# Squares in four listed slots, decays in six, and the last batch's input transposed before its gate: a gated recurrence and a gated convolution on one Trainium2 core

## Chip, cores, metric

One core of a Trainium2 chip. The metric is device time in microseconds (us). The engines are PE (TensorE, with PEld its weight loads), DVE (VectorE), ACT (ScalarE), POOL (GpSimd) and SP (SyncE, which here only issues DMAs). An operation is named by a short word and its numbers, as in the kernel's own list: `sc.25.0` is the scan of chunk 25, half 0.

## What is computed

x, r_gate and i_gate are [4, 6336, 256] in float32, with four small parameter arrays. Cut to what matters:

```python
a_t = exp(8 * sigmoid(r_gate) * log(sigmoid(a_param)))
x_gated = sqrt(max(1 - a_t * a_t, 1e-6)) * sigmoid(i_gate) * x
for t in range(S):                      # per batch row, all 256 channels
    h = a_t[:, t] * h + x_gated[:, t]
    y[:, t] = h
gate = sigmoid(causal_conv5(y, conv_w))  # depthwise, 5 taps
out = (gate * (y @ w_val)) @ w_out
```

## The kernel before

The 25,344 rows of the four sequences are one line of time. It is cut into 51 **windows** of 512 rows (the first two and the last have 256), and the windows into 28 **chunks**, mostly two windows each: chunk 24 is windows 45 and 46, chunk 25 is 47 and 48, chunk 26 is 49, chunk 27 is 50. Chunks are gathered in eight **batches** (`BATCHES`, L19), because the square root needs another table of ACT than tanh and exp: each batch costs two table loads. The last batch is chunks 25, 26 and 27.

Rows arrive with time on the partitions; the recurrence needs channels on the partitions, in two halves of 128 (`h`). For a chunk `c` or a window `w` the steps are:

- `lr`, `li`, `lx` (L279): SP loads a window of the r gate, the i gate and x, 512 KB each, into rings of four windows.
- `ta`, `tb` (L297, L300, ACT): tanh of half the gate, from which the sigmoid comes.
- `tr` (L344, PE) transposes tanh of the r gate, `ex` (L360, ACT) takes exp of it: the **decay** a_t, in float32, in `aring`.
- `sq` (L368, POOL) or `sa` (L376, ACT) squares the decay into `ering`. `rt` (L393, ACT) takes the square root of 0.25 - 0.25 a^2 over a whole batch, in as few instructions as there are contiguous pieces, and writes it as bf16 over the front half of the same piece.
- `pp` and `up` (L307, L319, POOL): 1 + tanh, and its product with x, written to `uring` in time-major order. For a few windows PE copies x to PSUM instead (`xp`, L324) and DVE does both steps in one (`uv`, L333).
- `nt` (L407, PE) transposes the root back to time-major order in PSUM; `xg` (L414, DVE) multiplies `uring` by it; `xt` (L422, PE) transposes the product, pairs of bf16 moved as one float32 word, to channel-major order in PSUM; `sc` (L444, DVE) scans it with the decays into `yring`.
- `cv` (L456, PE) is the convolution, 20 small matmuls a window; `tg` (L463, ACT) its tanh; `vl` (L471, PE) is y @ w_val; `gv` (L476, DVE) the gated product; `ou` (L486, PE) its product with w_out; `cd` (L494, DVE) or `ca` (L496, ACT) copies it to SBUF, `st` (L507) stores it.

So in the last batch the way from the root to the scan goes `rt`, `nt`, `xg`, `xt`, `sc`. The lines that say it (L411 to L427 and L430, shortened):

```python
def op_xg(c):
    ...
    nc.vector.tensor_tensor(out=u, in0=live.pop(("nT", c)).bitcast(BF16), in1=u, op=ALU.mult)
...
def op_sc(c, h):
    xT = live.pop(("xT", c, h)).bitcast(BF16)
```

**What sets the order.** `ORDER` (L35 to L98) is a list of 980 words written out ahead of time; the loop at L518 emits them one by one. Every engine takes its own instructions in the order of the list, and waits where data or a buffer are not ready. The numbers after an @ are the PSUM banks, eight in all, that a word uses. So a word that is moved in the list is moved on its own engine's queue, past what else stands there.

**The rings.** `aring` holds 5120 columns of each half, five chunks of 1024, used in turn. `ering` also holds 5120, and `places` (L138) hands out its slots in turn as well. A square can be written only when the root or the `nt` that used its slot has gone by.

Of the kernel before, what the change touches and what calls it, by code (L numbers as in the profile page):

```python
# [20 lines left out]
NA = 5120  # L21
NE = 5120
# [13 lines left out]
s_ident s_small s_kt s_diag lr.0 lr.2 lr.1 li.0 lr.3 ta.0 ta.2 lr.4 tr.0.1@5 ta.1 tr.2.0@4 ex.0.1 lr.5 tr.1.1@0  # L36
tr.2.1@7 ex.2.0 lr.6 sq.0.1 ex.1.1 li.2 ex.2.1 tr.0.0@0 tb.0 tr.1.0@7 ex.1.0 li.4 ex.0.0 lx.1 sq.1.0 ta.3 s_wl.3 sq.2.0
lx.0 li.3 sq.0.0 lx.3 ta.4 sq.1.1 li.1 sq.2.1 lx.2 lr.8 tb.2 tr.3.1@0,1 ex.3.1 tr.3.0@6,7 li.6 lr.9 xp.0@3 lr.7 uv.0
lx.4 ex.3.0 sq.3.1 s_wl.0 s_wl.2 tb.3 sq.4.1 lr.10 tb.1 xp.2@4,5 sq.3.0 xp.1@0 s_wl.1 uv.1 rt.0.0 li.8 sq.4.0 li.5 pp.3
nt.0@6 rt.1.0 nt.1@7 lx.6 xg.1 pp.4 xg.0 xt.0.1@2 sc.0.1 up.3 uv.2 xt.1.1@2 xt.1.0@3 nt.2@6 xg.2 up.4 lx.7 sc.1.1 lx.5  # L40
xt.2.0@7 ta.5 xt.0.0@0 xt.2.1@6 li.7 sc.0.0 nt.3@4,5 sc.1.0 s_wcast ta.6 xg.3 lr.11 cv.0@2,3 lr.12 sc.2.1 cv.1@4,5 tg.0
lr.14 tb.4 sc.2.0 lr.13 tr.5.1@0,1 vl.0@2,3 gv.0 tg.1 li.10 pp.6 ex.5.1 li.9 xt.3.1@4 lx.8 sc.3.1 up.6 tr.5.0@2,3
cv.2@6,7 ex.5.0 xt.3.0@1 pp.5 sc.3.0 tb.5 up.5 nt.4@2,3 vl.1@4,5 tg.2 gv.1 sq.5.0 lx.9 xg.4 ou.0.0@4 ta.7 li.11
ou.1.0@7 li.12 cd.1.0 xt.4.0@2 sq.6.1 cd.0.0 cv.3@6,7 ta.8 sc.4.0 st.0 lr.16 pp.7 st.1 tg.3 tr.7.0@0,1 lr.17 xt.4.1@5
up.7 ex.7.0 sc.4.1 vl.2@6,7 xp.8@2,3 tb.6 sq.5.1 lx.11 cv.4@0,1 gv.2 tg.4 uv.8 tr.7.1@4,5 li.14 sq.6.0 lr.15 ex.7.1
ou.2.0@6,7 lx.10 lr.18 vl.4@2,3 sq.7.0 cv.5@0,1 gv.4 tb.7 cd.2.0 sq.8.0 vl.3@4,5 tg.5 gv.3 xp.9@2,3 sq.7.1 lx.13 uv.9
ou.4.0@0,1 li.15 lx.12 rt.2.0 ou.3.0@4,5 li.13 sq.8.1 cd.3.0 vl.5@6,7 gv.5 pp.10 cd.4.0 ou.5.0@6,7 rt.2.1 up.10 cd.5.0
st.4 nt.5@4,5 xg.5 nt.6@2,3 pp.11 lx.14 li.16 xg.6 xt.5.1@0 pp.12 st.2 xt.5.0@6 st.3 sc.5.1 xt.6.1@7 up.11 cv.6@4,5
ta.10 sc.5.0 up.12 nt.7@2,3 ta.9 lr.21 lr.22 vl.6@0,1 tg.6 xg.7 lr.20 lx.15 tb.8 lr.19 sc.6.1 tr.9.0@4,5 xt.6.0@6 tb.9
li.18 tr.9.1@2,3 pp.14 lx.16 gv.6 xt.7.1@7 li.17 pp.13 ex.9.1 sc.7.1 li.19 cv.7@0,1 up.14 st.5 li.20 ex.9.0 sc.6.0  # L50
pp.15 vl.7@2,3 up.13 tg.7 ou.6.0@4,5 ta.12 cv.9@6,7 cd.6.0 up.15 gv.7 xt.7.0@4 tg.9 lr.25 lr.26 vl.8@0,1 sc.7.0 ta.11
st.6 pp.16 cv.8@2,3 lx.18 lx.17 sq.9.0 lx.19 tg.8 tr.11.0@6,7 ex.11.0 vl.9@4,5 gv.8 up.16 ou.7.0@2,3 gv.9 tb.10
nt.8@0,1 cd.7.0 sq.11.0 tr.11.1@6,7 xg.8 st.7 ex.11.1 ou.8.0@2,3 lx.20 pp.17 cd.8.0 xt.8.0@4 xt.8.1@5 sq.10.1 tb.11
cv.11@0,1 sc.8.1 st.8 lr.23 cv.10@2,3 lr.24 sq.10.0 tg.11 li.21 li.22 sc.8.0 tg.10 li.23 ou.9.0@0,1 sq.11.1 ta.14
cv.12@6,7 cd.9.0 sq.9.1 tg.12 lr.30 vl.11@4,5 gv.11 vl.12@2,3 pp.20 vl.10@0,1 gv.12 rt.3.0 sq.12.1 xp.18@4,5 gv.10
# [36 lines left out]
sq.27.0 pp.49 sc.24.1 cv.44@2,3 tg.43 pp.48 pp.50 vl.42@0,1 up.48 gv.42 rt.7.0 ou.41.0@6,7 vl.43@4,5 cd.41.0 up.47
# [10 lines left out]
def kernel(  # L103
# [82 lines left out]
    with tc.manual_schedule():  # L186
# [368 lines left out]
```

## Time and profile before

| | |
|---|---|
| median of 3 runs | 291.31 us (291.29 to 292.64) |
| the profiled execution: its time, its span | 293.39 us, 291.6 us |
| ACT busy in the span | 272.4 us (93%) |
| PE, DVE, POOL busy | 244.7, 243.5, 235.2 us (84, 83, 81%) |
| DMA | 104.75 MB, mean 359 GB/s |
| last root (chunks 25 to 27) | 261.26 to 264.45 us |
| last copy to SBUF ends, span ends | 288.13, 291.6 us |

The span is what the profiler shows of one execution, and that execution's own time is 1.8 us longer. All times in us below are positions in the span unless they are called the time. "Busy" counts overlapping instructions of one engine once. A row's mean is the mean duration of one instruction, which on ACT overlaps its neighbour a little: the sum of all rows' means of ACT is 285.8 us for 272.4 us busy. In a timeline a row merges neighbours of a kind; the bracket is the idle time before it and who ended it.

### The profile page before, as it was taken

What the parts mean: (1) busy time and instruction counts of PE and PEld (TensorE: products, weight loads), DVE (VectorE), ACT (ScalarE), POOL (GpSimd) and SP (SyncE); (2) the same over time, 40 slices, a digit from 0 to 9 for tenths busy, and PEclk for the clock granted to TensorE, in tenths of its full rate; (3) what the DMA queues carried; (4) which work ended last, traced back from release to release, by engine and by line L of the source; (5) the groups of instructions that cost most, each with busy time, mean ns of one, the idle gap of its engine ahead of it and who ended that gap; (6) DMA issues with size and microseconds to landing.
All of it is one profiled execution on the core that took longest, in us unless ns stands there. A gap on an engine that the chain in (4) does not pass through costs nothing. (4 is left out here: it accounts for less than half of the span.)

```text
span 291.6 us, 6228 instructions
## 1 busy us (share of the span) xinstructions
PE 244.7 (84%) x2482; PEld 168.5 (58%) x2507; DVE 243.5 (83%) x201; ACT 272.4 (93%) x191; POOL 235.2 (81%) x156
## 2 busy tenths in 40 slices
PE   1366697988689888899788789899999899999993
PEld 1242565556547456666457567566666577757662
DVE  2001799789999989998899989999999999999980
ACT  6799989999999999999999999999999999997663
POOL 1529949999599899999998999998999966898000
PEclk9997689999999999999999999999999999999999
DMA  7999999998999999899999999999999987782725
GB/s 239 316 386 405 383 407 385 380 371 333 395 411 418 416 415 366 285 418 416 418 416 416 411 411 416 419 388 378 416 416 420 415 326 276 267 288 110 290 87 239
DMA packets 29995, 104.75 MB, mean 359 GB/s; under 512 B 3335, under 2 KB 3854, under 8 KB 29966
## 3 DMA queue, kind: packets, MB, share of 16 engines
q1 hardware_dynamic: 29952, 104.35, 91.7%
q8 instruction: 19, 0.31, 0.4%
q14 instruction: 10, 0.08, 0.1%
q10 hardware_dynamic: 14, 0.01, 0.0%
HBM read 78.39 MB, written 25.95 MB: 358 GB/s over the span
## 5 line engine op out<-in xcount | busy, mean ns | idle before, releaser
L444 DVE TENSOR_TENSOR_SCAN yring<-aring,yring,banks 128x1024 bf16<-128x1024 f32 (+5 forms) x54 | 106.8, 1993 | 2.6 <-PE banks L422 1.3
L368 POOL TENSOR_TENSOR ering<-aring 128x1024 f32<-128x1024 f32 (+2 forms) x55 | 92.6, 1709 | 16.4 <-ACT aring L360 16.3
L319 POOL TENSOR_TENSOR uring<-tbring,xring 128x1024 bf16<-128x1024 bf16 (+1 forms) x45 | 95.3, 2136 | 1.5 <-DMA xring<-in_x_dram 0.8
L476 DVE SCALAR_TENSOR_TENSOR tgring<-tgring,banks 128x1024 bf16<-128x1024 bf16 (+1 forms) x51 | 59.3, 1181 | 7.8 <-PE banks L471 2.8
L456 PE MATMUL banks<-yring,diag 64*64 64x512 bf16 (+7 forms) x1080 | 63.2, 365 | 1.4 <-DVE tgring L476 0.4
L307 POOL TENSOR_SCALAR tbring<-tbring 128x1024 bf16<-128x1024 bf16 (+1 forms) x45 | 46.2, 1039 | 14.9 <-ACT tbring L300 14.8
L486 PE MATMUL banks<-wo,tgring 128*128 128x256 bf16 x396 | 50.5, 273 | 8.9 <-DVE tgring L476 6.2
L463 ACT ACTIVATE tgring<-banks 128x1024 bf16<-128x1024 f32 (+1 forms) x51 | 50.2, 1007 | 4.2 <-PE banks L456 4.1
L360 ACT ACTIVATE aring<-banks,khf 128x2048 f32<-128x2048 bf16 (+3 forms) x34 | 53.4, 1610 | 0.7 <-POOL ering L368 0.3
L471 PE MATMUL banks<-yring,wv 128*128 128x512 bf16 (+7 forms) x191 | 48.4, 359 | 4.9 <-ACT aring L360 1.6
L486 PEld LDWEIGHTS <-tgring 128*128 128x128 bf16 x396 | 42.3, 114 | 17.5 <-DVE tgring L476 7.6
L297 ACT ACTIVATE taring<-rring 128x2048 bf16<-128x2048 f32 (+2 forms) x28 | 47.7, 1722 | 1.9 <-DMA rring<-in_r_gate_dram 1.9
L300 ACT ACTIVATE tbring<-iring 128x2048 bf16<-128x2048 f32 (+2 forms) x28 | 48.0, 1727 | 0.3 <-DVE uring L333 0.3
L456 PEld LDWEIGHTS <-diag 64*64 64x64 bf16 x1080 | 30.3, 107 | 25.2 <-issue 9.7
L393 ACT ACTIVATE ering<-ering 128x2048 bf16<-128x2048 f32 (+4 forms) x11 | 44.1, 4042 | 0.1
L344 PE MATMUL banks<-ident_b,taring 128*128 128x128 bf16 x396 | 29.9, 230 | 12.0 <-ACT taring L297 8.3
L494 DVE COPY oring<-banks 128x1024 f32<-128x1024 f32 (+1 forms) x31 | 36.3, 1182 | 3.6 <-PE banks L486 3.5
L422 PE MATMUL banks<-ident,uring 128*128 128x128 f32 x198 | 30.8, 283 | 7.8 <-DVE uring L414 4.4
L344 PEld LDWEIGHTS <-taring 128*128 128x128 bf16 x396 | 25.5, 103 | 17.6 <-ACT taring L297 10.2
L471 PEld LDWEIGHTS <-wv 128*128 128x128 bf16 x216 | 19.5, 97 | 23.4 <-issue 10.0
L414 DVE TENSOR_TENSOR uring<-banks,uring 128x2048 bf16<-128x2048 bf16 (+2 forms) x28 | 30.2, 1092 | 2.5 <-PE banks L407 2.1
L422 PEld LDWEIGHTS banks<-ident,uring 128*128 128x128 f32 x198 | 22.0, 142 | 16.3 <-DVE uring L414 7.6
(37 smaller groups left out, 139.6 us busy)
## 6 DMA issues: line engine op xcount, KB each, us to landing
rring<-in_r_gate_dram SPq DMA_DIRECT2D x48, 512.0 KB, 8.2
iring<-in_i_gate_dram SPq DMA_DIRECT2D x48, 512.0 KB, 9.8
xring<-in_x_dram SPq DMA_DIRECT2D x48, 512.0 KB, 8.2
out_dram<-oring SPq DMA_DIRECT2D x48, 512.0 KB, 8.2
rring<-in_r_gate_dram SPq DMA_DIRECT2D x3, 256.0 KB, 3.8
iring<-in_i_gate_dram SPq DMA_DIRECT2D x3, 256.0 KB, 6.3
xring<-in_x_dram SPq DMA_DIRECT2D x3, 256.0 KB, 6.9
out_dram<-oring SPq DMA_DIRECT2D x3, 256.0 KB, 7.1
```

The lines of the kernel that those rows point to most:

```text
L300: nc.scalar.activation(**tangent(c, tbring, NTI, iring, NII))
L319: nc.gpsimd.tensor_tensor(out=u, in0=t1, in1=xt, op=ALU.mult)
L344: nc.tensor.transpose(out=bank[:, o:o + P], in_=taring[:, place(w, NTR), j, h * P:(h + 1) * P], identity=ident_b[:])
L360: nc.scalar.activation(out=dst, in_=src, func=ACT.Exp, scale=khf[:, h:h + 1], bias=khf[:, h:h + 1])
L368: nc.gpsimd.tensor_tensor(out=e, in0=a, in1=a, op=ALU.mult)
L422: nc.tensor.transpose(out=bank[:, o + q:o + wins[w] // 2:nq], in_=uring[:, (w + 1) % NU, q, h * P:(h + 1) * P, :].rearrange("p d two -> p ...
L444: nc.vector.tensor_tensor_scan(out=yring[:, h, col:col + o1 - o0], data0=aring[:, h, a_at[c] + o0:a_at[c] + o1], data1=xT[:, o0:o1], initi ...
L456: nc.tensor.matmul(out=gp[oh * 64:oh * 64 + 64, h, a:b], lhsT=diag[half * 64:half * 64 + 64, h, k, :], rhs=yring[half * 64:half * 64 + 64, ...
L463: nc.scalar.activation(out=tgring[:, w % NTG, :, 0:wins[w]], in_=live.pop(("gp", w))[:, :, 0:wins[w]], func=ACT.Tanh, scale=0.5)
L471: nc.tensor.matmul(out=val[:, m, a:b], lhsT=wv[:, hk, m * P:(m + 1) * P], rhs=yring[:, hk, col:col + b - a], start=(hk == 0), stop=(hk == ...
L476: nc.vector.scalar_tensor_tensor(out=tgring[:, w % NTG, :, 0:wins[w]], in0=tgring[:, w % NTG, :, 0:wins[w]], scalar=1.0, in1=live.pop(("va ...
L486: nc.tensor.matmul(out=ops[:, j * D:(j + 1) * D], lhsT=gv[:, hk, j:wins[w]:J], rhs=wo[:, hk, :], start=(hk == 0), stop=(hk == H - 1))
```

## The change

Four things are changed at once.

1. The ring of squares shrinks from five slots to four (`NE` 5120 to 4096), and the slots are listed (`SQUARES_AT`) and not handed out in turn. A batch of four chunks uses all four; a root now covers at most two neighbouring slots (`NPIECE`), so the batches 4, 5 and 7 take two root instructions where they took one. The root's result lies in the front slot of its pair.
2. The ring of decays grows from five chunks to six (`NA` 5120 to 6144). Both rings together take the same space.
3. For the chunks from 25 on (`DIRECT`) there is no `nt`. `xt` transposes the input before it is multiplied by the root, both halves in one word, and leaves it in PSUM; `xg` multiplies it there by the root, which is channel-major already, and writes the product to `uring` in SBUF; `sc` scans from SBUF.
4. `ORDER` is written anew throughout, 977 words. Counted by kind: `xp`/`uv` 6 to 3, `pp`/`up` 45 to 48 each, `nt` 28 to 25, `sq` 55 to 54, `sa` 1 to 2, `ca` 20 to 17, `cd` 31 to 34, `rt` 11 to 14. The table loads stay 14.

```diff
-NA = 5120
-NE = 5120
+NA = 6144
+NE = 4096
+NPIECE = 2048
+DIRECT = 25
+SQUARES_AT = [0, 256, 512, 2048, 3072, 1024, 0, 3072, 2048, 1024, 0, 3072, 2048, 1024, 0, 3072, 2048, 1024, 0, 3072,
+    2048, 1024, 0, 3072, 2048, 1024, 3072, 3584]
-    e_at = places(NE, clen)
+    e_at = SQUARES_AT
...
-            cs, got, k = BATCHES[b], [], 0
+            cs, got, k = sorted(BATCHES[b], key=lambda c: e_at[c]), [], 0
-                while m < len(cs) and e_at[cs[m]] == e_at[cs[m - 1]] + clen[cs[m - 1]]:
+                while m < len(cs) and e_at[cs[m]] == e_at[cs[m - 1]] + clen[cs[m - 1]] and e_at[cs[m]] % NPIECE:
...
+        def u_of(c):
+            u0, nw = (cwins[c][0] + 1) % NU, len(cwins[c])
+            return uring[:, u0:u0 + nw, 0:wins[cwins[c][0]] // (2 * P)].rearrange("p w q d two -> p (w q d two)")
+
         def op_xg(c):
+            u = u_of(c)
+            if c < DIRECT:
+                nc.vector.tensor_tensor(out=u, in0=live.pop(("nT", c)).bitcast(BF16), in1=u, op=ALU.mult)
+                return
+
+            o = 2 * live["n", c]
+            nc.vector.tensor_tensor(out=u, in0=live.pop(("uT", c)).bitcast(BF16),
+                                    in1=ering[:].bitcast(BF16)[:, o:o + H * clen[c]], op=ALU.mult)
+            for h in range(H):
+                live["xT", c, h] = u[:, h * clen[c]:(h + 1) * clen[c]]
...
+        def op_xt(c, *at):
+
+            if c < DIRECT:
+                h, b = at
+                words(c, h, banks[:, b])
+                live["xT", c, h] = banks[:, b].bitcast(BF16)
+                return
+            ps = banks[:, at[0]:at[-1] + 1].rearrange("p b n -> p (b n)")[:, 0:clen[c]]
+            for h in range(H):
+                words(c, h, ps[:, h * clen[c] // 2:(h + 1) * clen[c] // 2])
+            live["uT", c] = ps
```

The parts of the two lists that the prediction speaks of. Before, ACT's order up to the first root, and all words from the last root on:

```text
ta.0 ta.2 ta.1 ex.0.1 ex.2.0 ex.1.1 ex.2.1 tb.0 ex.1.0 ex.0.0 ta.3 ta.4 tb.2 ex.3.1 ex.3.0 tb.3 tb.1 rt.0.0
...
rt.7.0 ou.41.0 vl.43 cd.41.0 up.47 ou.42.0 gv.43 st.41 cv.45 cd.42.0 up.49 nt.25 tg.45 xg.25 vl.45 tg.44 vl.44 gv.45 up.50
xt.25.1 gv.44 ou.43.0 ca.43.0 ou.45.0 sc.25.1 xt.25.0 ca.45.0 st.43 ou.44.0 st.45 cv.46 ca.44.0 st.42 sc.25.0 st.44 tg.46
vl.46 nt.26 nt.27 xg.26 cv.47 xg.27 gv.46 xt.26.1 tg.47 xt.26.0 sc.26.1 vl.47 ou.46.0 sc.26.0 xt.27.1 ca.46.0 cv.48 gv.47
st.46 cv.49 tg.48 sc.27.1 tg.49 vl.48 xt.27.0 gv.48 ou.47.0 ca.47.0 sc.27.0 vl.49 gv.49 st.47 ou.48.0 cv.50 ca.48.0 tg.50
ou.49.0 st.48 ca.49.0 vl.50 gv.50 st.49 ou.50.0 ca.50.0 st.50
```

After, the same two parts:

```text
ta.0 ta.1 ex.0.0 ta.2 tb.0 ex.1.1 ex.0.1 ex.2.1 ex.1.0 ta.3 ex.2.0 ta.4 tb.2 tb.1 ex.3.0 ex.3.1 tb.3 ta.5 rt.0.0
...
xt.25 rt.7.0 gv.41 sq.26.1 vl.43 cv.45 up.49 gv.43 rt.7.1 xg.25 ou.42.0 cv.44 cd.42.0 tg.45 sc.25.1 ou.41.0 st.42 xt.26
ca.41.0 vl.45 tg.44 st.41 gv.45 vl.44 tb.27 vl.46 pp.50 xg.26 up.50 gv.44 ou.43.0 cv.46 ca.43.0 sc.25.0 st.43 tg.46 ou.44.0
ca.44.0 ou.45.0 gv.46 cv.48 ca.45.0 st.44 sc.26.1 cv.47 tg.48 sc.26.0 xt.27 tg.47 ou.46.0 xg.27 ca.46.0 sc.27.1 vl.48
sc.27.0 st.46 vl.47 gv.48 st.45 cv.49 gv.47 tg.49 ou.48.0 ca.48.0 vl.49 gv.49 st.48 ou.47.0 cv.50 ca.47.0 tg.50 ou.49.0
st.47 ca.49.0 vl.50 gv.50 st.49 ou.50.0 ca.50.0 st.50
```

More of the change, by code (lines that the diff above doesn't have):

```diff
@@ L39 @@
[L39 to L43, printed above, removed]
@@ new lines @@
+lr.6 tr.2.0@1 ex.1.1 tr.1.0@5 li.2 tr.2.1@6 ex.0.1 li.1 ex.2.1 sq.0.1 lx.0 ex.1.0 li.3 sq.1.1 ta.3 s_wl.1 sq.0.0 li.4
+pp.0 sq.2.1 ex.2.0 lr.7 s_wl.3 ta.4 sq.2.0 lr.8 lx.2 tb.2 tr.3.0@2,3 lx.1 up.0 tb.1 sq.1.0 lr.9 ex.3.0 tr.3.1@4,5 lx.3
+s_wl.0 ex.3.1 sq.4.0 s_wl.2 lr.10 tb.3 sq.3.1 lx.4 ta.5 li.6 sq.4.1 li.8 li.5 pp.1 xp.2@4,5 sq.3.0 rt.0.0 lx.6 uv.2
+li.7 lr.11 pp.3 rt.1.0 nt.2@7 lr.12 up.1 nt.0@4 nt.1@0 xg.0 xg.2 pp.4 lx.5 xg.1 xt.1.1@2 xt.1.0@7 up.4 xt.0.1@0
+xt.2.0@3 sc.0.1 xt.0.0@6 sc.0.0 sc.1.0 up.3 ta.6 nt.3@0,1 sc.1.1 cv.0@6,7 sc.2.0 lr.13 s_wcast tg.0 xg.3 lr.14
@@ new lines @@
+tr.5.1@4,5 tb.4 xt.2.1@6 cv.1@2,3 sc.2.1 xt.3.1@1 tg.1 li.10 pp.6 sc.3.1 ex.5.1 lx.7 cv.2@2,3 li.9 pp.5 lx.8 up.6 tg.2
+vl.0@4,5 vl.1@0,1 gv.0 tb.5 xt.3.0@7 gv.1 up.5 tr.5.0@2,3 sc.3.0 ou.0.0@6 ta.7 li.12 vl.2@0,1 li.11 ou.1.0@4 sq.5.1
+cd.0.0 ex.5.0 lr.15 gv.2 nt.4@6,7 sq.6.1 cd.1.0 cv.3@0,1 ta.8 xg.4 st.1 cv.4@4,5 sq.5.0 tg.3 lr.18 xt.4.0@6 lr.17 tg.4
+sc.4.0 lr.16 tr.7.1@2,3 sq.6.0 st.0 ex.7.1 lx.9 xp.7@4,5 pp.8 uv.7 tb.6 tr.7.0@0,1 up.8 xt.4.1@4 sc.4.1 ex.7.0
+ou.2.0@6,7 li.14 pp.10 vl.4@2,3 lx.12 lx.10 tb.7 li.13 gv.4 sq.8.0 cv.5@4,5 lx.11 cd.2.0 tg.5 vl.5@0,1 sq.7.1 ta.10
@@ new lines @@
+sc.15.1 ex.19.1 st.22 up.32 vl.24@4,5 lr.42 xt.16.0@7 ta.21 gv.24 vl.26@2,3 sq.20.0 cv.25@0,1 sc.16.0 tb.19 lr.44
+cv.27@4,5 lr.41 sq.19.1 lx.36 li.37 gv.26 tg.25 ou.24.0@6,7 li.40 sq.19.0 tg.27 cd.24.0 vl.27@0,1 xt.16.1@3 gv.27 st.24
+sq.20.1 vl.25@6,7 lr.43 rt.5.0 sc.16.1 ou.26.0@4,5 pp.34 ou.27.0@0,1 pp.33 gv.25 up.33 cd.27.0 rt.5.1 nt.17@2,3 cd.26.0
+ou.25.0@6,7 up.34 lx.37 cd.25.0 nt.18@4,5 xg.17 cv.30@0,1 pp.36 lx.38 li.39 xg.18 xt.17.0@6 tg.30 pp.35 xt.17.1@7
+sc.17.0 cv.29@2,3 ta.22 up.36 cv.28@4,5 tg.29 lr.46 sc.17.1 up.35 st.25 vl.30@0,1 tg.28 lr.45 tr.21.0@2,3 tb.20
@@ new lines @@
+nt.19@4,5 gv.30 ex.21.0 vl.28@6,7 li.41 pp.38 xg.19 st.27 tr.21.1@0,1 li.42 pp.37 gv.28 lx.39 vl.29@4,5 ex.21.1 lx.40
+sq.22.0 xt.18.1@3 gv.29 st.26 cv.31@6,7 sc.18.1 ta.23 up.38 xt.18.0@5 ou.28.0@0,1 tg.31 cd.28.0 vl.31@2,3 up.37 tb.21
+gv.31 ou.29.0@6,7 nt.20@0,1 sc.18.0 sq.22.1 ta.24 li.43 cv.32@2,3 st.28 pp.39 tg.32 lr.50 xg.20 ou.31.0@4,5 li.44
+ca.29.0 pp.40 cd.31.0 vl.32@2,3 tb.22 st.29 sq.21.0 tr.23.1@6,7 lx.42 gv.32 xt.19.0@5 st.31 lr.47 ex.23.1 sc.19.0
+ou.30.0@0,1 up.40 cv.33@2,3 tg.33 xt.19.1@7 cd.30.0 pp.42 lx.44 sa.21.1 tr.23.0@4,5 up.39 sc.19.1 st.30 ex.23.0
@@ new lines @@
+ou.32.0@2,3 li.46 cv.34@0,1 lx.41 cd.32.0 tg.34 sq.23.0 vl.33@6,7 xt.20.1@5 tb.23 gv.33 cv.36@0,1 pp.41 sc.20.1
+cv.35@6,7 ta.27 li.48 sq.23.1 li.47 tg.35 ou.33.0@2,3 cd.33.0 tg.36 vl.34@4,5 pp.43 vl.35@6,7 gv.34 st.33 sq.24.0
+xt.20.0@1 li.45 st.32 gv.35 rt.6.0 lx.43 ou.34.0@4,5 sq.24.1 sc.20.0 ou.35.0@2,3 vl.36@6,7 up.42 ca.35.0 gv.36
+nt.21@0,1 rt.6.1 cd.34.0 up.41 lx.46 nt.22@6,7 xg.21 st.34 cv.38@4,5 lr.48 pp.44 lr.49 xg.22 xt.21.1@0 xt.21.0@1 up.44
+sc.21.1 cv.37@2,3 tg.38 ou.36.0@6,7 up.43 lx.48 tg.37 sc.21.0 tr.27.1@0 lx.45 vl.37@4,5 ca.36.0 tb.24 st.36 gv.37 st.35
@@ new lines @@
+nt.23@6,7 xt.22.1@1 xt.22.0@3 xg.23 tb.25 pp.46 cv.39@4,5 sc.22.1 up.46 tg.39 ou.37.0@6,7 ex.27.1 cv.40@4,5 ca.37.0
+sc.22.0 pp.48 lx.50 li.49 tg.40 pp.45 lx.47 vl.38@0,1 xt.23.0@7 ta.25 sq.27.1 gv.38 vl.40@2,3 pp.47 tr.27.0@6 gv.40
+vl.39@4,5 ex.27.0 up.45 ta.26 tr.25.1@6 gv.39 ex.25.1 ou.38.0@0,1 tr.26.0@2 sc.23.0 ex.26.0 nt.24@4,5 sq.25.1 ca.38.0
+tr.25.0@6 ex.25.0 ou.39.0@2,3 st.38 xg.24 xt.23.1@7 lx.49 ca.39.0 sq.25.0 ou.40.0@0,1 sc.23.1 tr.26.1@6 ca.40.0
+xt.24.0@2 xt.24.1@3 ex.26.1 st.40 cv.41@0,1 up.48 li.50 tb.26 sc.24.0 st.37 cv.42@6,7 tg.41 st.39 up.47 cv.43@4,5
@@ L148 @@
     a_at = places(NA, clen)
-    e_at = places(NE, clen)
+    e_at = SQUARES_AT
+    assert all(e + n <= NE for e, n in zip(e_at, clen))
     segs, y_at, y_wrap = [], [], []
@@ L409, in op_nt, with words @@
             live["nT", c] = bank[:, 0:k]
+        def u_of(c):
+            u0, nw = (cwins[c][0] + 1) % NU, len(cwins[c])
+            return uring[:, u0:u0 + nw, 0:wins[cwins[c][0]] // (2 * P)].rearrange("p w q d two -> p (w q d two)")
         def op_xg(c):
-            u0, nw = (cwins[c][0] + 1) % NU, len(cwins[c])
-            u = uring[:, u0:u0 + nw, 0:wins[cwins[c][0]] // (2 * P)].rearrange("p w q d two -> p (w q d two)")
-            nc.vector.tensor_tensor(out=u, in0=live.pop(("nT", c)).bitcast(BF16), in1=u, op=ALU.mult)
-        def op_xt(c, h, at):
-            bank = banks[:, at]
+            u = u_of(c)
[7 more added lines that the diff above has]
+                live["xT", c, h] = u[:, h * clen[c]:(h + 1) * clen[c]]
+        def words(c, h, out):
             for w in cwins[c]:
@@ L422, in op_xt @@
                     nc.tensor.transpose(
-                        out=bank[:, o + q:o + wins[w] // 2:nq],
+                        out=out[:, o + q:o + wins[w] // 2:nq],
                         in_=uring[:, (w + 1) % NU, q, h * P:(h + 1) * P, :].rearrange("p d two -> p (d two)")
```

93 lines of the change are left out of this document (33 added, 60 removed).

## Prediction

> **What bounds the kernel now.** I read the page's busy times first, then the stretches, the waits, the timeline of the tail and the chain that ended last.
>
> ```profile
> PE 244.7 (84%) x2482; PEld 168.5 (58%) x2507; DVE 243.5 (83%) x201; ACT 272.4 (93%) x191; POOL 235.2 (81%) x156
> ```
>
> ACT has least room, but this is an average over unlike stages, so I cut the span: the middle, and the tail from the start of the last root.
>
> ```profile
> 49.45:261.26 211.81, 190.22 (x2016) 131.96 (x2030) 200.25 (x153) 210.46 (x140) 197.40 (x123) 1.00 0.98 383
> 261.26:288.20 26.94, 25.19 (x251) 16.99 (x252) 22.58 (x21) 18.59 (x17) 7.29 (x4) 1.00 0.49 198
> ```
>
> The columns are time, then busy time of PE, PEld, DVE, ACT, POOL, then PE's granted clock, the DMA's share, GB/s. In the middle ACT is busy 210.5 of 211.8 us: it sets the pace. DVE has 11.6 us of room, POOL 14.4; the DMA's share is 0.98. In the tail ACT has room and PE has not: 25.2 of 26.9, DVE 22.6. The timeline shows the turn:
>
> ```profile
> 261.26 3.19 ACT L393 ACTIVATE ering<-ering 128x3584 bf16<-128x3584 f32 x1
> ...
> 264.77 1.23 PE L407 MATMUL banks<-ident,ering 128*128 128x128 f32 x8
> ...
> 266.11 1.23 DVE L414 TENSOR_TENSOR uring<-banks,uring 128x2048 bf16<-128x2048 bf16 x1 [0.35 <-PE banks L407]
> ```
>
> The root's way through `nt` to `xg.25` takes 4.85 us (261.26 to 266.11), yet DVE waits only 0.35 for it: it had other work. So the shorter way (no `nt`) is worth little as latency. What counts is work taken from PE, and when ACT reaches the last root. The chain that ended last is PE alone from 237.3 to 286.0, which agrees.
>
> **The change, part by part.** Durations are row means; for a queue I sum them and scale by what the queue took (neighbours overlap): ACT 210.5 us for 222.3 of means, 0.947; DVE 0.961; POOL 0.983.
>
> *Start.* ACT's first root moves behind `ta.5` (one 1.92 us tanh); against that stand waits of 1.89, 0.18 and 0.32 us in this stretch, the first (for `lr.6`) mostly filled by `ex.2.0`, and ACT's order otherwise holds the same work. I put the root at 27.5 (26.07 before). `xp.0`, `xp.1` go, so PE has only `xp.2` behind it, and I count its next transposes at the slow row:
>
> ```profile
> 28.21 0.60 PE L407 MATMUL banks<-ident,ering 128*128 128x128 f32 x4
> ...
> 31.52 1.06 PE L407 MATMUL banks<-ident,ering 128*128 128x128 f32 x4
> ...
> 34.48 1.91 PE L407 MATMUL banks<-ident,ering 128*128 128x128 f32 x8
> ```
>
> Four take 0.60 us when PE had just been busy for 4.54 us with `xp` (granted clock 0.98 there) and 1.06 at a clock of 0.50 later. Root to 29.4, eight such to 31.4, products 32.5, then transposes of 0.33 each and five scans to about 36.4, `cv.0` 1.28: `tg.0` at 37.7, as before (37.66). Then nine ACT instructions, 13.1 us before; with about 0.9 of waiting of `tg.1` and `tg.2` for late convolutions `ta.8` ends at 51.7 (before 47.02 + 3.73 = 50.75): **+1.0 us**, and -0.5 if the clock is full. DVE, by the same walk, has done `xg.4` at 50.9. The Trainium skill (TensorE: Matmul & The Clock Gate, What's actually happening) has PE at half rate until about 3.4 us of sustained work; the clocks here agree, and by it the slow row is right for this start.
>
> The doubled POOL work for windows 0 and 1 (`pp` 0.62, `up` 1.18 each, 3.6 us) falls into POOL's early idle time (6.43 and 5.49 us of waits for ACT's exp).
>
> *Middle, ACT.* From `ta.8` to the last root ACT has less to do: four copies fewer ahead of it (12 to 8, -4.1), `tb.27` now behind it (-0.66), two root pieces more (a root is 0.20 + 0.835 per 1000 columns by its rows 1906 and 7035 ns: +0.4), `sa.21.1` and `sa.27.0` for `sa.26.1`. No row has a Square of 1024 or 256 columns: the first lies between 0.73 (512 columns) and 1.24 (exp of 1024), the second between 0 and 0.57 (exp of 256); taken 1.17 and 0.50, together +0.9. Sum -3.4, by 0.947 **-3.3 us** (ends -3.9 and -3.2). So the last root starts at 51.7 + 207.3 = 259.0 (261.26).
>
> *What may not follow.* DVE loses three `uv` pairs (1.47 for a pair or two short ones) less one gained, and gains three copies of 1.22. With no waiting it would reach the last root's place at 250.6 before (49.45 + 209.3 x 0.961), 10.7 ahead of ACT, and at 50.9 + 210.4 x 0.961 = 253.1 after, 5.9 ahead of 259.0. It loses 4.8 us of lead; ACT's tanh then waits more often for convolutions. Nothing shows how much: ends 0 and 4.8, I take a quarter, **+1.2**, because ACT waited under 1 us in the middle with the lead it had.
>
> POOL gains in the middle `pp` and `up` of one window (3.2) less a square (1.9). Its idle time there came in waits for `tb` after roots (4.74, 3.50 us), and the new order puts `tb` nearer to the root: cover enough. With four slots a next batch's squares can't begin before the root, but the root frees the back slot of each pair at once; the list puts them later still: nothing. The loads must come 2 us earlier; the DMA ran at 333 to 385 GB/s from 44 to 73 us and at 326 or less from 233 us on, against 416 at best: nothing.
>
> *Tail.* From the last root on PE had 25.05 us by the chain's pieces (`ou` 0.87, `vl` 0.86, `cv` 1.21, a transpose of `nt` 0.122, of `xt` 0.14). `nt` goes (14 x 0.122 = -1.7), `xt.25` is ahead of the root (-1.1), `cv.44` behind it (+1.2): 23.4, **-1.6 us**. The rest of 26.87 us from the root to the last copy (1.8) and the store behind it (3.5) I leave. The root comes in two parts, so `xg.25` needs 1.9 us of it, not 3.2. The scans from SBUF: every scan in the trace reads PSUM (2338 ns); those of chunks 25 to 27 are 8.5 us together. Bounds from the nearest rows: `xg` at 1215 ns for 2048 shows that DVE has no general loss with an operand in PSUM, so between -0.3 (0.05 each) and +0.3; taken 0.
>
> Sum: +1.0 - 3.3 + 1.2 - 1.6 = **-2.7 us**. The profiled execution would take 290.7 where it took 293.39; its time was 2.1 above the median, so from the median 291.31 - 2.7 = **288.6 us**.
>
> **Rivals.**
>
> *DVE takes over the bound* (slower). After 50.9 it has 232.9 x 0.961 = 223.8 us to do, 222.8 after 49.45 before, and then 1.3 us of `ou.50` and copy remain. Before, it waited 14.5 us on the way, mostly under 1 us at a time for its own last product to come back through PE, which the change does not shorten. With the same waits the last copy ends at 50.9 + 223.8 + 14.5 + 1.3 = 290.5, +2.4: 293.7. It decides once DVE's waits pass 12.1 us. For it: the waits are by PE and ACT after DVE's own results. Against it: DVE had 11 us in hand because ACT was slow.
>
> *All of it comes through*: clock full at the start, no loss of DVE's lead: -0.5 - 3.3 - 1.6 = -5.4, 285.9. Against it: the clock rows.
>
> *Only the tail comes*: the lost lead eats the middle: -1.6, 289.7.
>
> *POOL is late for `xt.25`*. That word now stands ahead of `vl.43` on PE and needs `up.47` and `up.48`. POOL can reach the end of `up.47` at 38.8 (its weight casts' end: 36.1 before, plus most of the four early instructions added) + 213.0 x 0.983 = 248.2 plus its waits; with the 13.7 us of before that is 261.9, 2.9 after the root, and PE stands: -2.7 + 2.9, 291.5. For it: PE takes its queue in order. Against it: the nearer `tb`.
>
> *DVE and POOL exclude each other in the tail.* The scans from SBUF read two SBUF tiles, which no scan before did, and `up.49` (2.16 us) and `up.50` (1.18) may run beside them: up to 3.3 us, of which DVE's room against PE in the tail (25.2 less 21.6 of work and 1.3 behind it, some 2) covers most: +1.3, 289.9. No row shows such a pair in the middle, for or against. The Trainium skill (SBUF — State Buffer, Who interferes with whom) says that a DVE instruction with two SBUF inputs blocks against a GpSimd one that reads SBUF; by that rule it would happen wherever they overlap.
>
> **How the numbers follow.** Forecast 0.37, with 287.4 to 290.0 as its own range; DVE bound 0.20; all comes through 0.13; only the tail 0.12; POOL late 0.10; exclusion 0.08. About 0.5% (1.46 us) is what a measurement of this kernel can tell from no change: below 289.85 is faster, above 292.77 slower. Faster: 0.34 of the forecast, 0.13, half of the tail case and of the exclusion: 0.57. Slower: 0.20. Same: the rest, 0.23. The range runs from the middle of "all comes through" to nearly that of "DVE bound", 286.0 to 293.4, leaving out some 0.07 below and 0.11 above.
>
> **What would show it.** In the changed profile: the first root near 27.5 and `ta.8`'s end near 51.7; the last root near 260 in two pieces; PE busy over 23 us between it and the last copy, in 25; DVE's waits after 51 us at 8 to 11. I am wrong if ACT shows waits of several us in the middle (DVE bound), if PE waits at `xt.25` on POOL, or if scans of the last chunks or `up.50` take well over their rows.

## Result and the profile after

| | before | after |
|---|---|---|
| median of 20 runs each, interleaved | 293.0 us | 291.16 us |
| ratio, 95% interval | | 0.9938 (0.9914 to 0.9961) |
| profiled execution: time, span | 293.39, 291.6 us | 291.52, 289.7 us |

The changed kernel is faster by 0.6%, 1.84 us between the medians and 1.87 between the profiled executions (the interval does not reach 1, but the gain is small). Forecast were 2.7. (The three runs of before that were shown first lie in the lower part of its twenty; that is why 291.16 stands so near to the 291.31 of the prediction.) The size alone misleads, though: two of the three parts of the sum came out on the other side of zero from the forecast. In the experiments below a median is over all runs of a kernel, a ratio over the runs in the faster of the two states that its executions show.

| us in the span | before | after | forecast |
|---|---|---|---|
| first root starts | 26.07 | 26.00 | 27.5 |
| `tg.0` starts | 37.66 | 34.72 | 37.7 |
| `ta.8` ends | 50.75 | 47.81 | 51.7 |
| last root starts | 261.26 | 260.43 | 260.2 |
| last copy ends | 288.13 | 286.76 | |
| start: up to `ta.8` | | -2.94 | +1.0 |
| middle: `ta.8` to the last root | 210.51 | 212.62, +2.11 | -2.1 |
| tail: last root to the last copy | 26.87 | 26.33, -0.54 | -1.6 |
| store behind it | 3.47 | 2.94, -0.5 | 0 |

The middle of before, cut at the end of `ta.8` (columns as in the prediction):

```profile
50.75:261.26 210.51, 188.93 (x1994) 131.30 (x2017) 198.95 (x152) 209.16 (x140) 196.10 (x122) 1.00 0.98 383
```

The busy times of after, then its middle and its tail:

```profile
PE 240.9 (83%) x2485; PEld 163.7 (57%) x2485; DVE 243.2 (84%) x200; ACT 271.1 (94%) x192; POOL 240.5 (83%) x161
```

```profile
47.81:260.43 212.62, 189.91 (x1987) 129.90 (x1984) 201.40 (x152) 206.36 (x138) 200.05 (x122) 0.99 0.99 386
260.43:286.76 26.33, 24.49 (x257) 15.09 (x255) 21.61 (x21) 20.20 (x20) 5.30 (x5) 1.00 0.45 181
```

ACT's work in the middle fell nearly as forecast, from 209.2 us busy to 206.4 (-2.8 for -3.3). The stretch grew all the same: ACT now stands idle 6.3 us in it, 1.4 before. The waits tell where. ACT in the timeline of after:

```profile
113.43 2.06 ACT L364 ACTIVATE aring<-banks,khf 128x2048 f32<-128x2048 bf16 x1 [0.68 <-DVE yring L469]
...
174.67 2.06 ACT L364 ACTIVATE aring<-banks,khf 128x2048 f32<-128x2048 bf16 x1 [2.18 <-DVE yring L469]
...
182.75 1.02 ACT L488 ACTIVATE tgring<-banks 128x1024 bf16<-128x1024 f32 x1 [1.03 <-PE banks L511]
```

and DVE in the same places, with what it was waiting for itself:

```profile
115.53 2.35 DVE L469 TENSOR_TENSOR_SCAN yring<-aring,yring,banks 128x1024 bf16<-128x1024 f32 x1 [1.01 <-ACT aring L364]
...
122.91 2.35 DVE L469 TENSOR_TENSOR_SCAN yring<-aring,yring,banks 128x1024 bf16<-128x1024 f32 x1 [1.50 <-ACT aring L364]
...
172.22 2.33 DVE L469 TENSOR_TENSOR_SCAN yring<-aring,yring,banks 128x1024 bf16<-128x1024 f32 x1
...
182.76 1.23 DVE L519 COPY oring<-banks 128x1024 f32<-128x1024 f32 x1 [3.01 <-PE banks L511]
```

The first two ACT rows are exp instructions (L364) that wait for a scan (L469), and DVE's first two are scans that wait for an exp. In before, no exp waited for a scan: all of ACT's waits from 50 us to the last root were under 1 us together. Take the one at 174.67. It is `ex.19.1`, which writes the decays of chunks 19 and 20. The scan that ends just before it, 172.22 to 174.55, is `sc.15.1` by the order of the list. In a ring of six, chunks 19 and 20 lie in the last slot and the first, which chunks 13 and 14 had; chunk 15 has the second slot, which this exp does not touch. That is the trail.

### The profile page after: what moved, and what is told of

Read it like the earlier page. It is cut to its first block, busy times and chain, and to the rows that moved or that the text cites. A ratio compares the mean times of both kernels' runs of the same rounds, so it can differ in the third digit from the quotient of the medians.

```text
span 289.7 us, 6214 instructions
## 1 busy us (share of the span) xinstructions
PE 240.9 (83%) x2485; PEld 163.7 (57%) x2485; DVE 243.2 (84%) x200; ACT 271.1 (94%) x192; POOL 240.5 (83%) x161
## 4 chain that ended last, share of the span: by engine, by line
ACT 30%; PE 23%; DMA 18%; DVE 15%; issue 12%; SPq 1%; ACTq 0%; DVEq 0%
PE banks L481 7%; PE banks L511 6%; ACT taring L301 6%; DMA xring<-in_x_dram 6%; ACT aring L364 6%; DMA iring<-in_i_gate_dram 6%; DMA rring<-in_r_gate_dram 6%; DVE yring L469 5%; PE banks L496 5%; ACT tgring L488 5%; ACT ering L397 5%; ACT tbring L304 4%; DVE oring L519 4%; DVE tgring L501 3%; ACT L548 2%
## 5 line engine op out<-in xcount | busy, mean ns | idle before, releaser
L323 POOL TENSOR_TENSOR uring<-tbring,xring 128x1024 bf16<-128x1024 bf16 (+1 forms) x48 | 100.0, 2098 | 3.8 <-DMA xring<-in_x_dram 3.2
L469 DVE TENSOR_TENSOR_SCAN yring<-aring,yring,banks 128x1024 bf16<-128x1024 f32 (+5 forms) x48 | 98.0, 2058 | 4.6 <-ACT aring L364 2.5
L311 POOL TENSOR_SCALAR tbring<-tbring 128x1024 bf16<-128x1024 bf16 (+1 forms) x48 | 48.7, 1023 | 11.5 <-ACT tbring L304 11.4
L364 ACT ACTIVATE aring<-banks,khf 128x2048 f32<-128x2048 bf16 (+3 forms) x34 | 53.4, 1600 | 3.2 <-DVE yring L469 2.9
L496 PE MATMUL banks<-yring,wv 128*128 128x512 bf16 (+4 forms) x216 | 50.4, 364 | 4.2 <-ACT aring L364 3.5
L511 PEld LDWEIGHTS <-tgring 128*128 128x128 bf16 x396 | 41.4, 114 | 17.4 <-issue 8.1
L481 PEld LDWEIGHTS <-diag 64*64 64x64 bf16 x1080 | 29.4, 108 | 28.9 <-issue 12.9
L519 DVE COPY oring<-banks 128x1024 f32<-128x1024 f32 (+1 forms) x34 | 39.8, 1182 | 5.8 <-PE banks L511 4.7
L397 ACT ACTIVATE ering<-ering 128x4096 bf16<-128x4096 f32 (+2 forms) x14 | 44.5, 3218 | 0.1
L411 PE MATMUL banks<-ident,ering 128*128 128x128 f32 x184 | 27.4, 296 | 9.8 <-ACT ering L397 5.7
L411 PEld LDWEIGHTS banks<-ident,ering 128*128 128x128 f32 x184 | 24.1, 207 | 14.7 <-ACT ering L397 6.4
```

Of the source, the lines that this page charges most:

```text
L323: nc.gpsimd.tensor_tensor(out=u, in0=t1, in1=xt, op=ALU.mult)
L364: nc.scalar.activation(out=dst, in_=src, func=ACT.Exp, scale=khf[:, h:h + 1], bias=khf[:, h:h + 1])
L397: nc.scalar.activation(out=ering[:].bitcast(BF16)[:, 4 * o:4 * o + 2 * n], in_=ering[:, 2 * o:2 * o + 2 * n], func=ACT.Sqrt, scale=-0.25, ...
L469: nc.vector.tensor_tensor_scan(out=yring[:, h, col:col + o1 - o0], data0=aring[:, h, a_at[c] + o0:a_at[c] + o1], data1=xT[:, o0:o1], initi ...
L481: nc.tensor.matmul(out=gp[oh * 64:oh * 64 + 64, h, a:b], lhsT=diag[half * 64:half * 64 + 64, h, k, :], rhs=yring[half * 64:half * 64 + 64, ...
L496: nc.tensor.matmul(out=val[:, m, a:b], lhsT=wv[:, hk, m * P:(m + 1) * P], rhs=yring[:, hk, col:col + b - a], start=(hk == 0), stop=(hk == ...
```

## Experiments

Two theories of the middle. **The strided pair:** an exp does two chunks at once. Where the pair lies in the last and the first slot of `aring`, its output is one pattern with a stride over the whole ring (the `else` of `op_ex`), and what orders the accesses treats all that lies between as written. The exp then waits for the scans of the chunks between, and scans of these wait for it. In six slots this meets the pairs 7/8, 13/14 and 19/20; in the five of before 11/12 and 21/22. **The rival, DVE's lost lead,** is the prediction's: DVE has less in hand, and ACT waits for it wherever a buffer comes round.

### The middle: the strided pair

**e1** turns the ring by one slot, so that no pair is split:

```diff
-    a_at = places(NA, clen)
+    a_at = [(a - 1024) % NA for a in places(NA, clen)]
```

> The changed kernel with the ring of decays turned by one slot (chunk 3 at column 0, so that no pair of chunks lies in the last and the first slot); nothing else differs. In the changed kernel the exp of such a pair (chunks 7 and 8, 13 and 14, 19 and 20) is written with one strided pattern that spans the ring, and waits for scans of chunks between. Theory A (these waits are false and cost the middle its gain): ACT's waits between 48 and 260 us fall from 5.8 to under 2 us, DVE's waits of 1.0, 1.5 and 3.0 us go, the last root starts at 256.5 to 258.5 (260.4 in the changed kernel), the time is 2 to 4 us below the changed kernel's (ratio to the kernel before 0.980 to 0.987, the changed kernel's was 0.994). Theory B (DVE's own pace took the gain): other waits take their place, last root within 1 us of 260.4, ratio 0.991 to 0.996.

Measured 285.2 us, 0.9762 (0.9726 to 0.9798) of before; span 283.0. All that ACT still waited for from 47 us to the last root, by the list of waits of e1 (in total, times, longest), and its middle and tail:

```profile
ACT tgring L488 <- PE banks L481: 0.4, 1, 0.4
ACT taring L301 <- DMA rring<-in_r_gate_dram: 0.2, 1, 0.2
```

```profile
47.48:253.94 206.46, 187.74 (x1987) 129.35 (x1984) 201.08 (x152) 205.48 (x138) 199.66 (x122) 1.00 1.00 396
253.94:279.91 25.97, 24.49 (x257) 15.10 (x255) 21.61 (x21) 20.18 (x20) 5.31 (x5) 1.00 0.43 173
```

The reader compares the row of the middle with that of after: the same instructions (x152 on DVE, x138 on ACT, x122 on POOL), 206.46 us in place of 212.62. That is 6.2 us less, more than the 2 to 4 expected: 5.3 of it is ACT's idle time (6.3 to 1.0), 0.9 its busy time. DVE has as much work as in after (201.08 and 201.40 us), and ACT hardly waits.

**e7** leaves the slots of after and writes a split pair's exp as two instructions of one chunk each:

```diff
-                dst = aring[:, h].rearrange("c (k n) -> c k n", n=n)[:, at[0] // n:at[1] // n + 1:(at[1] - at[0]) // n]
-                dst = dst.rearrange("c k (q j) -> c k q j", j=J)
+                for g, a in enumerate(at):
+                    nc.scalar.activation(out=aring[:, h, a:a + n].rearrange("c (q j) -> c q j", j=J), in_=src[:, g],
+                                         func=ACT.Exp, scale=khf[:, h:h + 1], bias=khf[:, h:h + 1])
+                return
```

> The changed kernel with its ring as it is, but the exp of the three pairs that lie in the last and first slot given as two instructions, one for each chunk, so that no pattern spans the ring. That is 6 more instructions on ACT, some 0.3 to 0.42 us each by the rows (1.24 for 1024 columns against 2.07 for 2048), 1.8 to 2.5 us. If the strided pattern is the cause (theory A): no wait of exp for scans of chunks between, last root at 255.7 to 257 (253.9 with the turned ring, 260.4 in the changed kernel), ratio to the kernel before 0.980 to 0.988. If the position in the ring is (theory B): last root at 262 or later, ratio above 0.995.

Measured 286.35 us, 0.9788 (0.975 to 0.9826); the last root starts at 256.77, 3.7 earlier than in after. `ta.8` ended later than in after (49.44), so the middle took 207.33 us, 5.3 less than in after. All that ACT waited for in it, by the list of waits of e7:

```profile
ACT tgring L490 <- PE banks L483: 0.4, 1, 0.4
```

The slots and the true needs are those of after, so it is the one strided instruction that cost the time. The median is 1.15 us above e1's: each of the six split instructions costs ACT about 0.24 us more (2.30 us for two of 1024 columns, 2.06 for one of 2048), 1.4 in all.

**e8** does the same to the kernel before, which has two such pairs.

> The kernel before, with the exp of its two wrapped pairs (chunks 11 and 12, 21 and 22) in two instructions each. Its trace shows no wait of exp for a scan over 0.3 us, so theory A: nothing to win, four more instructions on ACT at 0.3 to 0.42, ratio 1.003 to 1.007. If its pairs cost it hidden time as the changed kernel's do: ratio under 0.998.

Measured 293.02 us, 1.0022 (0.9992 to 1.0052): nothing was to be had there. The flaw stood in the code before the change, but no exp of the trace of before waits for a scan, so the scans between had been done when the exp came. The change moved the place of the pairs and the order at once; which of the two made the flaw bite is not separated.

**e2** is after with five decays, as before had.

```diff
-NA = 6144
+NA = 5120
```

> The changed kernel with five slots of decays (NA 5120) as before; order and all else as changed. If the sixth slot carries the gain (exp may run a chunk further ahead of the scans): ACT waits for scans in more places, some 1 to 4 us more, ratio to the kernel before 0.998 to 1.008. If it does not matter, or costs as much by its three wrapped pairs (two with five slots) as it brings: ratio within 0.002 of the changed kernel's 0.994, or below it.

Measured 292.72 us, 1.001 (0.9983 to 1.0038). ACT waits 5.1 us for scans. **e9** asks whether these are the false kind: e2 and e7's edit together.

> The changed kernel with five decay slots (as in e2, 292.72) and with the exp of a wrapped pair written as two instructions. It tells whether the ACT waits of e2 (1.58, .68, .27, .57, 2.00 us, all for scans) are true, for a slot that is not yet read, or false ones of the strided pattern. True waits of a full ring: the time stays at 292 to 293.5. False ones: it falls by the sum of them, about 5 us, to 287 to 288.

Measured 293.25 us, 1.002 (0.9985 to 1.0056): no gain. The lists of ACT's waits in the middle, e2 first, then e9 (where L363 is the exp of one chunk, L366 the exp of a whole pair):

```profile
ACT aring L364 <- DVE yring L469: 5.1, 5, 2.0
```

```profile
ACT aring L366 <- DVE yring L471: 3.5, 4, 2.0
ACT aring L363 <- DVE yring L471: 1.5, 2, 1.1
```

The waits are still there, 5.0 us, with no strided pair left: four of the six, 3.5 us, are at exps of pairs that were never split, and the other two at single chunks that need their own slots. So with five slots in this order the ring is truly full, and without strided pairs the sixth slot is worth 2.6% (e1, 0.9762, against e9, 1.002). In the change as made, the strided pairs took all but 0.7% of it back (0.9938 against 1.001). The kernel before with six decays was not tried, so what the slot is worth in the old order is open.

### The start

**e4** puts windows 0 and 1 back on PE and DVE (`xp.0 uv.0 xp.1 uv.1` in the places of `pp` and `up` 0 and 1), with the rest of after.

> The changed kernel with the input products of windows 0 and 1 done as before, by PE (copy to PSUM) and DVE, and not by POOL. Theory A (taking them off PE and DVE is what made the start early: the first convolution's tanh at 34.7 us, 37.7 before): that tanh goes back to 36.2 to 37.7 us, and the time grows by 0.5 to 2 us, as far as the lead isn't lost in the middle anyway. Rival (the start is early because of the order of the loads and of ta.5): the tanh stays within 0.7 us of 34.7.

Measured 293.6 us, 1.0021 (0.9988 to 1.0055), 0.8% above after by the ratios. Its timeline, PE at the first root's transposes and at `cv.0`:

```profile
29.64 1.33 PE L411 MATMUL banks<-ident,ering 128*128 128x128 f32 x8
...
35.49 1.28 PE L481 MATMUL banks<-yring,diag 64*64 64x256 bf16 x20
```

and the same two in after:

```profile
27.96 1.18 PE L411 MATMUL banks<-ident,ering 128*128 128x128 f32 x8 [0.61 <-ACT ering L397]
...
33.93 0.74 PE L481 MATMUL banks<-yring,diag 64*64 64x256 bf16 x20
```

In e4 `ex.3.1` waits 1.13 us for its transposes (none in after), the first root starts at 27.23 and `tg.0` at 36.83; in after at 26.00 and 34.72. Of the 2.9 us that the start won, 2.1 are these two windows', and they come through to the end: the last copy ends at 289.00, 2.2 later than in after. The granted clock at `cv.0` is 0.50 in e4 and 1.00 in after (34 to 36 us), beside 1.28 and 0.74 us.

### The tail

**e3** is after with chunk 25 done the old way (`nt`, `xg`, `xt` into PSUM, scanned there), in banks that later words of the list need.

> The changed kernel with chunk 25 alone done the old way (its root transposed back by PE, product, transposed again, scan from PSUM); chunks 26 and 27 stay direct. Theory A (PE bounds the tail, what counts is PE's work): 8 transposes of 0.122 us more after the last root and 8 of xt (1.1 us) moved behind it, so the way from the last root to the last copy grows from 26.3 by 1.0 to 2.1 us. Rival (DVE bounds the tail, or the tail's end is set by the last window alone): it grows by less than 0.4 us.

Measured 299.76 us, 1.0272 (1.0225 to 1.0319); the tail took 36.95 us. PE's waits in it:

```profile
269.71 0.60 PE L511 MATMUL banks<-wo,tgring 128*128 128x256 bf16 x4 [2.00 <-DVE yring L469]
280.12 2.89 PE L511 MATMUL banks<-wo,tgring 128*128 128x256 bf16 x16 [2.44 <-DVE yring L469]
```

These are `ou.41` and `ou.44`: their banks hold the scan's input until the scan has read it. Behind each of the two stops PE's granted clock reads 0.50 to 0.72 for some 4 us (270 to 274, 280 to 284). So this run prices mostly the choice of banks and not the old way. **e5** mends that, on e1: the same, with `ou.41`, `vl.44`, `ou.44`, `ou.45` and `xt.26` in other banks.

> The kernel with the turned ring (283.0 us span, 26.0 us from the last root to the last copy), with chunk 25 alone done the old way as in the earlier run, but with the banks given out anew, so that no product of windows 41 to 45 waits for a bank that a scan of chunk 25 still reads. Theory A (PE bounds the tail, its work counts): 1.0 us more for 8 transposes of the root and 1.1 for 8 of xt behind the root: 27.0 to 28.1 us. Theory B (what cost 10 us in the earlier run was the banks, and the direct way is worth little else): under 26.6 us. If the tail is again above 30 us, the old way itself is that dear here.

Measured 288.64 us, 0.9863 (0.9827 to 0.99), 1.0% above e1 by the ratios, 2.5 us in the span of the profiled executions (285.5 and 283.0). The last root came 0.73 us earlier in e5 (253.21), but the tail took 29.35 us for 25.97. That is more than the 27.0 to 28.1 expected of PE's work alone. All that PE waited for in it:

```profile
PE banks L411 <- ACT ering L397: 1.7, 1, 1.7
PE banks L511 <- DVE tgring L501: 1.2, 1, 1.2
```

No bank is among these waits. PE is busy 1.3 us more than in e1 (25.80 and 24.49), stands 1.65 for the root ahead of `nt.25`, and waits 0.4 longer for the last `gv` (1.21 and 0.85): together the 3.4 us. So against this old way the direct way is worth some 3 us for chunk 25, half of it work of PE and half the way from the root. That half hangs on the order: before, PE had other words ahead of `nt.25` and did not wait. The banks, with the place of `xt.25.0`, are the difference of the tails of e3 and e5, 36.95 and 29.35 us.

### Do scans from SBUF and GpSimd exclude each other?

In after they hardly meet: every scan from SBUF took its usual time (2.34 us for 1024 columns, 2.34 from PSUM before). Three kernels make them meet. Each is e1 with useless POOL work added behind `up.49` and behind `up.50`. **e6** has eight products in float32 that read SBUF twice:

```diff
+        def op_zz(k):
+            r = rring[:, k % NRI].rearrange("p j d -> p (j d)")
+            nc.gpsimd.tensor_tensor(out=ering[:, 0:1024], in0=r, in1=r, op=ALU.mult)
```

> The kernel with the turned ring, and eight more products on GpSimd (1024 float32 read from SBUF, 1.9 us each) laid over the tail, two behind up.49 and six behind up.50; they write a slot of squares that is no longer read. So GpSimd reads SBUF while the scans of chunks 25 to 27 read two SBUF tiles. If a DVE instruction with two SBUF inputs and a GpSimd one exclude each other: scans of 1024 go from 2.34 us to up to 4.2, or the GpSimd products from 1.9 to as much as 4.2, and the way from the last root to the last copy grows from 26.0 by 2 to 6 us. If they do not: scans within 3% of 2.34, 1.27 and 0.74 us and the way within 0.4 us of 26.0.

Measured 291.22 us, 0.9935 (0.9901 to 0.9969); the span is 7.6 us longer than e1's, 6.0 between the medians. DVE in e6, and two answers for POOL in the same stretch:

```profile
264.84 2.91 DVE L473 TENSOR_TENSOR_SCAN yring<-aring,yring,uring 128x1024 bf16<-128x1024 f32 x1
...
268.79 1.73 DVE L473 TENSOR_TENSOR_SCAN yring<-aring,yring,uring 128x512 bf16<-128x512 f32 x1
...
270.49 2.79 DVE L473 TENSOR_TENSOR_SCAN yring<-aring,yring,uring 128x512 bf16<-128x512 f32 x1
```

```profile
265.55 3.88 POOL L376 TENSOR_TENSOR ering<-rring 128x1024 f32<-128x1024 f32 x1
...
269.51 5.46 POOL L376 TENSOR_TENSOR ering<-rring 128x1024 f32<-128x1024 f32 x2
```

The same scans in e1:

```profile
263.80 2.35 DVE L469 TENSOR_TENSOR_SCAN yring<-aring,yring,uring 128x1024 bf16<-128x1024 f32 x1
...
267.17 1.28 DVE L469 TENSOR_TENSOR_SCAN yring<-aring,yring,uring 128x512 bf16<-128x512 f32 x1
...
268.42 1.27 DVE L469 TENSOR_TENSOR_SCAN yring<-aring,yring,uring 128x512 bf16<-128x512 f32 x1
```

The rows fit turns taken whole. The scan of 264.84 comes while `up.50` still runs (264.43 to 265.61), and lasts 2.91 us for 2.35, so the kernel's own product holds a scan off too. A product alone takes 1.89 us. The one of 265.55 stands until the scan of 264.84 is done at 267.75, and ends 1.68 later, at 269.43; the scan of 268.79 stands until then, and ends 1.09 later; and so on. The scans took 5.7 us more in all. In the same trace DVE's products with one operand in PSUM kept their rows (1.20, 0.68, 0.39), and three scans from PSUM at 246.80 took 6.81 us with POOL at work beside them, as in e1.

**e10** has 18 memsets, which only write SBUF, in place of the products.

> e1 with extra GpSimd work beside the scans of the last chunks, as in e6, but 18 memsets of 1024 columns that only write SBUF in place of eight products that read it twice. If it is reading SBUF on GpSimd that excludes a scan with two SBUF inputs, scans of chunks 25 to 27 stay at e1's 2.34, 1.27 and 0.74 us and the time stays within 1 us of e1's 285.2. If any access of GpSimd does it, scans of two short chunks take over 2 us each as in e6 (2.79, 2.06), and the time is 289 to 292, if the memsets last as long as the scans run.

Measured 285.78 us, 0.976 (0.9731 to 0.9788). The scan that stands at 270.49 in e6, here at 268.75, and the memsets that ran beside it:

```profile
268.75 1.27 DVE L472 TENSOR_TENSOR_SCAN yring<-aring,yring,uring 128x512 bf16<-128x512 f32 x1
```

```profile
264.25 14.10 POOL L375 MEMSET ering<- 128x1024 f32 x14
```

No scan lost anything. **e11** has 18 additions with one float32 input.

> As e10, with 18 additions of a constant that read one SBUF input and write SBUF, in float32. If one input is enough to exclude, scans take 2 us and more where they were 1.27 and 0.74, and the time is 289 to 293. If only an instruction of GpSimd with two inputs excludes, scans keep e1's rows and the time stays within 1 us of 285.2.

Measured 314.33 us, 1.0738 (1.0707 to 1.0769), and neither expectation is answered by it: one addition takes 2.77 us alone, which I had not known, so POOL itself works until 311 and ends last. The rows answer in part. DVE, then POOL:

```profile
258.01 2.34 DVE L473 TENSOR_TENSOR_SCAN yring<-aring,yring,uring 128x1024 bf16<-128x1024 f32 x1
...
263.18 3.00 DVE L473 TENSOR_TENSOR_SCAN yring<-aring,yring,uring 128x1024 bf16<-128x1024 f32 x1
```

```profile
268.71 1.43 POOL L311 TENSOR_SCALAR tbring<-tbring 128x512 bf16<-128x512 bf16 x1
```

The scan of 258.01 began 1.2 us into an addition (256.80) and lost nothing; that of 263.18 began 0.2 us into one (263.00) and lost 0.66. POOL's `pp` of 268.71, with one input, began 0.25 us into a scan (268.46 to 269.73) and took 1.43 us where it takes 0.62. So one input is enough to be held off, as far as these two rows can show it. That an addition holds a scan off only in its first 0.84 us or so fits the rows; it is not shown further.

## Why the prediction was right and wrong

**Direction right, sum of wrong parts.** The forecast -2.7 was made of +1.0, -2.1 and -1.6. Measured: -2.9, +2.1, -0.5, and -0.5 behind the last copy. The parts miss by -3.9, +4.2, +1.1 and -0.5. That the last root starts within 0.3 us of the forecast 260.2, and that the sum lands within 1 us of its own, is luck: errors cancel.

**Start: the step that failed is the first root at 27.5, with the slow clock behind it.** ACT took `ta.5` ahead of the root, as said (+1.92). The prediction named waits of 1.89, 0.18 and 0.32 against it, but its 27.5 credits only some 0.5 of these 2.4. In the run 1.60 came off: the wait for the r gate fell to 0.79 (at 13.82), the two others are gone. ACT's first tanh also began 0.32 earlier in this execution (5.12 for 5.44), and the root at 26.00. From the root to `tg.0` forecast were 10.2 us, and 8.7 were measured: the slow row for PE did not hold. The eight transposes took 1.18 us at a granted clock of 1.00 from 24 to 30 us, with 0.57 only from 30 to 34; before, the clock was 0.50 from 32 to 38. From `tg.0` to the end of `ta.8` 13.1 us went by as before, without the 0.9 of waiting that was added. These three, -1.5, -1.5 and -0.9, are the whole miss; the prediction's term for a full clock, -0.5, was too small. On the Trainium skill's rule that was cited (TensorE: Matmul & The Clock Gate, What's actually happening: half rate until some 3.4 us of sustained work) this case gives no clean verdict: PE did nothing from 18.52 to 23.97, and the granted clock reads 1.00 all the same from 14 to 30 us.

**Middle, ACT's work: right.** Forecast -3.3. In e1, where nothing else disturbs it, the stretch is 4.05 us shorter than before, 3.7 of it ACT's busy time (209.16 to 205.48).

**Middle, "What may not follow": failed, and this is the main error.** It looked for the loss in DVE's lead, at +1.2, and named one sign: waits of several us on ACT. The sign came, 5.8 us, but not from there. By the waits of e1, DVE's lost lead cost ACT nothing to speak of (0.6 us of waits in all). The loss was the strided pair, 6.2 us, which the prediction did not see. Its sum has no term for the sixth decay slot: it asked neither what the slot frees (the 5 us of waits of e9) nor which pairs it splits; `op_ex` was in the code, and the three pairs could have been counted. "DVE takes over the bound" looks like what happened (DVE's waits after 50 us were 14.6, over its 12.1), yet e1 refutes it: DVE has the same work there, waits 8.3 and the last root comes 6.5 us sooner. In after, at the split pairs, DVE and ACT each waited for the other over slots they did not share; `vl.26` on PE stood 2.97 us too, because `ex.19.1` had yet to read its banks.

**Tail: PE's 23.4 was near, the end was not.** In both kernels PE works without a wait from the root to the end of `vl.50`: that took 24.74 us before (261.26 to 286.00) and 23.88 after (260.43 to 284.31), so -0.9 where the pieces gave -1.6 (25.05 to 23.4). Two terms were lacking, 0.5 us together: `ou.41`, which began 0.39 ahead of the root before (260.87), stands wholly behind it after, and the last 0.15 of `xt.25` does too. From there to the last copy's end are 2.45 us for 2.13, because the last `gv` starts 0.46 behind `vl.50`, not 0.10; that I had left as it was. Half a microsecond more came behind the last copy, in the store; why is not shown. The scans from SBUF cost what they did from PSUM: taken 0, measured 0. The prediction held the shorter way to be worth little as latency. In the order of before that stands; in that of after, e5 shows 1.65 us of PE standing for the root when `nt.25` is put back, and e3 shows what it costs when a scan then also holds the banks.

**The other rivals.** POOL was not late: `xt.25` started at 259.71, ahead of the root, and PE did not wait for it. The exclusion did not come in this kernel, because `up.49` and `up.50` ran beside products and all but clear of the scans. But e6 shows it to be real. The Trainium skill's rule (SBUF — State Buffer, Who interferes with whom), that a DVE instruction with two SBUF inputs contends with a GpSimd instruction that reads SBUF and not with one that only writes it, agrees with e6 and e10. The same section of the Trainium skill speaks of an exclusive lock, which the turns in e6 fit.

**All of it comes through** was put at 285.9 with 0.13. With the pairs unsplit it is 285.2, by other parts than were added up: the start brought 3.3 us (`ta.8` ends at 47.48), not 0.5, and the tail 0.9, not 1.6.

## What to carry to other kernels

When a ring changes its size, look at every instruction that takes several slots at once, find where it now wraps, and treat a strided output over the ring as touching all that it spans: a turn of one slot was worth 6.2 us of the middle here, and 1.8% by the ratios, three times the change itself. An engine's idle time that grows while its work shrinks is the sign; read who it waited for, find that instruction in the order, and ask whether the two share a byte. And give a PSUM bank back before a long reader, not after it: what stands behind the bank pays.

## What the runs showed of the hardware

- A scan with two SBUF inputs and a GpSimd product that reads SBUF go one after the other: up to 1.5 us on a scan of 1.27 (e6). Memsets beside the same scans cost nothing (e10).
- A scan runs as fast from SBUF as from PSUM: 2.34 us for 1024 columns both ways.
- GpSimd's addition of a constant to 1024 float32 columns took 2.77 us, its product of such a tile with itself 1.89, and its two-step operation on 1024 bf16 columns (`pp`) 1.04: the one with fewer inputs was not the shorter one.
